# Attention and two mixture layers on one core: another order of the first tiles' sums, queries and keys, and weight splitting handed to VectorE

## The chip, the cores and the metric

The kernel runs on 1 core of one Trainium2 chip. The metric is the device time of one execution in microseconds (us), the median of several runs. The five engines named below are TensorE (PE; PEld is its weight load), VectorE (DVE), ScalarE (ACT), GpSimd (POOL) and SyncE (SP, which here only issues DMAs).

## What is computed

```python
q_pool = q.reshape(B, H, S // 2, 2, D).mean(axis=3)            # B=2, H=8, S=1152, D=64
scores = np.matmul(q_pool, k.transpose(0, 1, 3, 2)) / np.sqrt(D)
attn = np.exp(scores - scores.max(-1, keepdims=True))
attn = attn / (attn.sum(-1, keepdims=True) + 1e-09)
x = np.matmul(attn, v)                                         # (2, 8, 576, 64)
x = x.transpose(0, 2, 1, 3).reshape(B * 576, H * D)            # 1152 tokens x 512
h = x @ w_in                                                   # 512 x 2048
x = np.maximum(0.01 * h, h) @ w_out                            # 2048 x 512
p = domain_probs / (domain_probs.sum(-1, keepdims=True) + 1e-09)
out = sum(p[:, e:e+1] * (np.maximum(x @ w1[e], 0) @ w2[e]) for e in range(4))
```

All is float32. TensorE works on a rounded type, so each operand is split into a high part (a rounded copy) and a low part (what the copy left), and a product is the sum of two or three matmuls.

## The kernel before, in words

**One instruction stream for each engine, written by hand.** The program runs under a manual schedule: every engine executes its instructions in the order in which the Python code calls them, and waits on semaphores where data or a buffer is not there yet. An instruction that waits therefore holds up everything behind it on its engine.

**Attention.** There are 8 pairs (a batch and two heads), each with 9 tiles of 128 pooled queries, so 72 tiles. A tile i goes through these steps:

- S (`emit_s`): TensorE, six matmuls 128x384 (L355), or twelve in pair 0's fifth tile, which needs both heads. They fill PSUM banks 0 to 2, and there is only one such buffer: the next tile's S waits until VectorE has read this one.
- VectorE scales the scores into SBUF tile e (five buffers) and takes the row minimum in the same instruction (L358).
- ScalarE's exp, with the row sum (`emit_exp`, L364).
- VectorE's two small steps: sum + 1e-9 (`emit_sum`, L368), then the reciprocal (L372 in `emit_norm`).
- GpSimd multiplies e by it (L374); in the last two tiles VectorE does.
- T (`emit_t`): TensorE transposes e in nine blocks (L395) through banks 3 to 5, three blocks a bank; ScalarE copies each bank to th (L399) and VectorE the rest to tl (L101).
- attention times v (L422), taken from a queue by `run_av` between other work. A finished chunk of 256 or 320 queries is added up (L430, L431) into xf and split into xh and xl (L94 or L96, and L101).

TensorE transposes tile i after it has issued S of tile i+2 (from tile 6 on of tile i+3). What comes before a tile's T is `upto("sum")`; the reciprocal and the normalisation stand inside `emit_t`, behind the first third of tl.

**Keys and queries.** For pair 0 (`first_pair`), both are loaded piece by piece: q_add pools the query pairs (L257), q_hi and q_lo split them, k_hi and k_lo the keys. For later pairs (`prep_pair`), q_add (L292), k_hi, k_lo, q_hi and q_lo run on GpSimd and ScalarE some tiles ahead. GpSimd's k_lo takes one instruction rk 128x1152; behind it SyncE issues four key DMAs (L288, L289), and behind q_lo four query DMAs into qst (L304).

**Weights.** The first feed-forward layer runs over 16 slices f of w_in, 36 matmuls 128x384 each (L190 to L192), and ends in `evac_leaky` (ScalarE's leaky ReLU into gf, L589, ScalarE's high part, VectorE's low part of 128x1152). `split64` splits a slice of weights that come as 64-bit words: s0 on ScalarE (L113), s1 VectorE (L116), s2 VectorE (L120), s3 VectorE (L127), ScalarE (L128) and one subtraction (L130), s4 (L134 on VectorE or L136 on GpSimd), s5 an addition (L139). Its argument `fast` says who does these: with 0 GpSimd does L130, L136 and L139 and ScalarE one more product (L122); with 1 VectorE does L134, GpSimd L130 and L139; with 2 VectorE does all three. `prep_a` splits w_in into tiles a, `prep_b` w_out into tiles b. Slices 0 and 1 of w_in are split during the last pair's tiles (`ahead`, AT0), slice 2 after attention, slice f+2 during slice f. What follows (w_out, and the four experts) the change does not touch.

Of the kernel before, what the change touches and what calls it, by code (L numbers as in the profile page):

```python
# [27 lines left out]
CW = 384  # L28
# [10 lines left out]
def tile_kernel(ctx: ExitStack, tc: tile.TileContext, q, k, v, w_in, w_out, probs, w1, w2, out):  # L39
# [130 lines left out]
    def prep_b(f, tmp):  # L170
        h, l = b_t[f] = tuple(b_b[f % 8][:, i] for i in range(2))
        return split64(h, l, wb_raw[f % 2].rearrange("p (a b) -> p a b", b=2), tmp, 1)
# [23 lines left out]
    with ExitStack() as actx:  # L196
# [76 lines left out]
        def prep_pair(n):  # L273
# [55 lines left out]
        P0, P1, P2 = 11, 1, 8  # L329
# [3 lines left out]
        AT0 = (0, 6)  # L333
# [116 lines left out]
        with tc.manual_schedule():  # L450
# [36 lines left out]
            for c in range(3):  # L487
                k_lo(DVE, 1, c * CW, (c + 1) * CW)
# [398 lines left out]
```

## Time and profile before

| | |
|---|---|
| median of 3 runs | 844.21 us (843.22 to 845.43) |
| profiled execution | 844.05 us |
| its span, first to last instruction | 842.0 us |
| mean granted TensorE clock | 0.996 of full speed |
| PE busy | 820.8 us (97%) |
| PEld busy | 775.6 us (92%) |
| DVE busy | 574.1 us (68%) |
| ACT busy | 434.5 us (52%) |
| POOL busy | 417.3 us (50%) |
| chain that ended last | PE 89%, DVE 7%, issue 2%, ACT 1%, POOL 1%, DMA 1% |

The shares are over the whole span, and the stages differ much: the last two thirds are nearly TensorE alone. A row of a timeline reads: start, duration, engine, line, operation, tile written and tiles read, shape, how many alike in a run; in brackets the idle time of the engine before it and what ended this. Times count from the start of the span, which is 2 us less than the execution.

### The profile page before, as it was taken

The page shows a single profiled execution, that of the slowest core. Times are in us where ns is not written, and L with a number is a line of the kernel's source. Part 1 is how long each engine was busy: PE and PEld are TensorE (multiplying, and loading weights), DVE is VectorE, ACT ScalarE, POOL GpSimd, SP SyncE. Part 2 cuts the span into 40 slices and gives each one's busy share as a digit, 9 for nine tenths or more (in the row PEclk, how much of TensorE's full clock was granted, in tenths as well). Part 3 has the DMA queues.
Part 4 walks back from the last instruction along what each step waited for, and adds up shares of the span by engine and source line. Part 5 has one row for each costly group of instructions (what it writes and reads, how often), then busy time and mean ns, then how long its engine had stood idle before and what let it go on. Part 6 is the DMA issues. An engine that isn't in the chain of part 4 may idle for free.

```text
span 842.0 us, 13590 instructions
## 1 busy us (share of the span) xinstructions
PE 820.8 (97%) x5091; PEld 775.6 (92%) x5091; DVE 574.1 (68%) x947; ACT 434.5 (52%) x764; POOL 417.3 (50%) x366
## 2 busy tenths in 40 slices
PE   6899999999989899999999999999999999999998
PEld 5799999999989799999999998989898998989897
DVE  5889999999998979767765762736445363625332
ACT  5889999999976555433432641505142341506030
POOL 3788888888753678556561240506042331504020
PEclk9999999999999999999999999999999999999999
DMA  7347644563401233331130120302011110201012
GB/s 224 90 132 189 181 105 136 162 174 96 138 26 52 100 100 101 100 99 52 51 101 26 51 76 1 100 1 88 13 51 51 50 52 4 98 0 52 0 38 100
DMA packets 25713, 68.65 MB, mean 82 GB/s; under 512 B 2992, under 2 KB 7856, under 8 KB 25648
## 3 DMA queue, kind: packets, MB, share of 16 engines
q1 hardware_dynamic: 25424, 67.43, 26.8%
q8 instruction: 40, 0.66, 0.3%
q10 hardware_dynamic: 224, 0.36, 0.1%
q14 instruction: 25, 0.20, 0.1%
HBM read 48.91 MB, written 2.36 MB: 61 GB/s over the span
## 4 chain that ended last, share of the span: by engine, by line
PE 89%; DVE 7%; issue 2%; ACT 1%; POOL 1%; DMA 1%; SPq 0%; DVEq 0%; POOLq 0%; ACTq 0%
PE ps L713 21%; PE ps L355 9%; PE ps L758 8%; PE ps L760 8%; PE ps L759 8%; PE ps L422 7%; PE ps L395 7%; PE ps L612 4%; PE ps L610 4%; PE ps L611 4%; PE ps L192 3%; PE ps L191 3%; PE ps L190 3%; DVE e L358 2%; DVE tl L101 1%
## 5 line engine op out<-in xcount | busy, mean ns | idle before, releaser
L101 POOL TENSOR_TENSOR bb<-w2r,bb 128x512 fp32r<-128x512 f32 x32 | 40.8, 1297 | 259.0 <-ACT bb L94 259.0
L767 DVE SCALAR_TENSOR_TENSOR oacc<-ps,pw,oacc 128x512 f32<-128x512 f32 (+1 forms) x64 | 47.5, 742 | 100.4 <-PE ps L760 100.4
L101 DVE TENSOR_TENSOR tl<-ps,th 128x384 fp32r<-128x384 f32 (+1 forms) x240 | 112.2, 505 | 3.2 <-ACT th L399 2.8
L758 PE MATMUL ps<-bb,gg 128*128 128x512 f32 (+1 forms) x292 | 112.9, 387 | 0.0
L760 PE MATMUL ps<-bb,gg 128*128 128x512 f32 (+1 forms) x292 | 112.8, 386 | 0.0
L759 PE MATMUL ps<-bb,gg 128*128 128x512 f32 (+1 forms) x292 | 112.8, 386 | 0.0
L713 PE MATMUL ps<-yT,ws 128*128 128x288 f32 x768 | 111.3, 296 | 0.0
L374 POOL TENSOR_SCALAR e<-e,st 128x1152 f32<-128x1152 f32 x70 | 86.3, 1234 | 42.8 <-DVE st L372 25.2
L713 PEld LDWEIGHTS ps<-yT,ws 128*128 128x128 f32 x768 | 105.6, 188 | 0.9 <-ACT cb L730 0.3
L358 DVE TENSOR_SCALAR_CACHE_REDUCE e<-ps 128x1152 f32<-128x1152 f32 x72 | 97.5, 1355 | 11.0 <-PE ps L355 9.7
L355 PE MATMUL ps<-k,qst 128*128 128x384 f32 x438 | 94.4, 346 | 7.9 <-DVE e L358 3.8
L399 ACT CAST th<-ps 128x384 fp32r<-128x384 f32 (+1 forms) x240 | 91.4, 459 | 17.9 <-PE ps L395 16.3
L719 ACT COPY ca<-ps 128x576 f32<-128x576 f32 x16 | 10.3, 641 | 167.1 <-PE ps L713 155.3
L364 ACT ACTIVATE e<-e,st 128x1152 f32<-128x1152 f32 x72 | 91.3, 1268 | 4.8 <-DVE e L358 2.8
L395 PE MATMUL ps<-ident,e 128*128 128x128 f32 x648 | 83.9, 275 | 5.1 <-POOL e L374 3.4
L355 PEld LDWEIGHTS ps<-k,qst 128*128 128x128 f32 x438 | 75.6, 190 | 13.0 <-DVE e L358 6.9
L713 PE MATMUL ps<-yB,ws 128*128 128x288 f32 x576 | 84.4, 296 | 0.0
L395 PEld LDWEIGHTS ps<-ident,e 128*128 128x128 f32 x648 | 75.1, 141 | 9.7 <-POOL e L374 5.1
L713 PEld LDWEIGHTS ps<-yB,ws 128*128 128x128 f32 x576 | 79.6, 188 | 0.6
L192 PE MATMUL ps<-xh,a 128*128 128x384 f32 x192 | 65.1, 339 | 2.8 <-POOL a L139 2.8
L190 PE MATMUL ps<-xh,a 128*128 128x384 f32 x192 | 64.8, 338 | 0.7 <-ACT gf L589 0.7
L760 PEld LDWEIGHTS ps<-bb,gg 128*128 128x128 f32 x292 | 54.9, 188 | 11.4 <-DVE gg L739 0.2
(126 smaller groups left out, 1724.9 us busy)
## 6 DMA issues: line engine op xcount, KB each, us to landing
wa<-in_w_in SPq DMA_DIRECT2D x16, 512.0 KB, 3.4
wb<-in_w_out SPq DMA_DIRECT2D x16, 512.0 KB, 4.3
wf<-in_w SPq DMA_DIRECT2D x32, 256.0 KB, 2.8
w2r<-in_w SPq DMA_DIRECT2D x16, 512.0 KB, 3.4
qst<-rq SPq DMA_DIRECT2D x28, 288.0 KB, 4.6
rv<-in_v SPq DMA_DIRECT2D x8, 576.0 KB, 6.6
rk<-in_k SPq DMA_DIRECT2D x7, 576.0 KB, 6.0
rq<-in_q SPq DMA_DIRECT2D x7, 576.0 KB, 5.3
```

What stands on the lines that cost most here:

```text
L101: eng.tensor_tensor(dst, src, f32(high), op=ALU.subtract)
L190: PE.matmul(ps[:, c, :CW], wh[:, k_], src_h[:, k_, cs], start=k_ == 0, stop=False)
L192: PE.matmul(ps[:, c, :CW], wl[:, k_], src_h[:, k_, cs], start=False, stop=k_ == KD - 1)
L355: PE.matmul(ps[:, c, :CW], x, y, start=m == 0, stop=m == len(mms) - 1)
L358: DVE.tensor_scalar(e, ps[:, :, :CW], -0.5 / float(D) ** 0.5, None, op0=ALU.mult, op1=ALU.min, accum_out=st[:, 0:1])
L364: ACT.activation(e, e, AF.Exp, bias=st[:, 0:1], scale=-1.0, accum_out=st[:, 1:2])
L395: PE.transpose(ps[:, j], e[:, (3 * g + j) * 128:(3 * g + j + 1) * 128], ident)
L399: ACT.copy(h, ps[:, :, s0:s0 + w])
L713: PE.matmul(ps[:, c, :HW], w[wi][:, i, ks], y[:, yi, k, c * HW:(c + 1) * HW], start=bool(first and k == 0 and m == 0), stop=k == 1 and m = ...
L758: PE.matmul(ps, gh[:, ts_], wh, start=f == fs[0], stop=False)
L759: PE.matmul(ps, gh[:, ts_], wl, start=False, stop=False)
L760: PE.matmul(ps, gl[:, ts_], wh, start=False, stop=f == fs[-1])
```

## The change

Three parts. **The first nine tiles:** pooling, q_hi and q_lo of pair 0 are cut into 128 and 320 columns, the first of which GpSimd subtracts; q_lo of head 1 goes from VectorE to GpSimd; of head 1's three key parts two move behind tile 2's scaling; the sums and reciprocals are called earlier (`sums`, `norms`), in tiles 0, 2 and 3 ahead of the next S; pair 1 is prepared one tile earlier, its queries ahead of its keys, with q_lo and its DMAs before k_lo. **The last pair:** GpSimd normalises all tiles; each slice of w_in has a list of tiles at which its six steps are called (a negative number is a tile before the last pair); slice 2 joins the list; one dummy Lrelu loads ScalarE's table three tiles before the end. **Weights:** `prep_b` gets `fast`; slices 1 to 4 of w_in and 0 and 1 of w_out are split with fast=2. TensorE's instructions and their order are the same in both kernels.

```diff
-    def prep_b(f, tmp):
+    def prep_b(f, tmp, fast):
...
-        return split64(h, l, wb_raw[f % 2].rearrange("p (a b) -> p a b", b=2), tmp, 1)
+        return split64(h, l, wb_raw[f % 2].rearrange("p (a b) -> p a b", b=2), tmp, fast)
...
-                return [[lambda: v_hi(0)], [lambda: v_lo(0)], [], [lambda: v_hi(1)], [], [lambda: v_lo(1)]]
+                return [[lambda: v_hi(0)], [lambda: v_lo(0)], [], [], [lambda: v_hi(1)], [lambda: v_lo(1)]]
             qk = [[q_add, k_hi], [k_lo], [q_hi], [q_lo, lambda: load_qk(n + 1)]]
+            if n == 1:
+                qk = [[q_add], [k_hi, q_hi], [q_lo, k_lo, lambda: load_qk(n + 1)], [], []]
...
-        P0, P1, P2 = 11, 1, 8
+        P0, P1, P2 = 11, 0, 8
-        AT0 = (0, 6)
+        AT0 = ((-3, -2, 0, 2, 3, 4), (6, 7, 7, 8, 9, 9), (8, 10, 10, 11, 11, 11))
...
-            eng = POOL if i < len(tiles) - 2 else DVE
-            eng.tensor_scalar(e, e, st[:, 3:4], 1.0, op0=ALU.mult, op1=ALU.mult)
+            POOL.tensor_scalar(e, e, st[:, 3:4], 1.0, op0=ALU.mult, op1=ALU.mult)
...
-            q_add(POOL, 0, 128, SQ)
+            for a, z in ((128, 256), (256, SQ)):
+                q_add(POOL, 0, a, z)
+            q_hi(0, 128, 256)
             upto("s", emit_s, 0)
-            q_hi(0, 128, SQ)
+            q_lo(POOL, 0, 128, 256)
+            q_hi(0, 256, SQ)
             keep_warm(10)
             upto("exp", emit_exp, 0)
-            q_lo(DVE, 0, 128, SQ)
+            q_lo(DVE, 0, 256, SQ)
...
             upto("s", emit_s, 1)
-            for c in range(3):
-                k_lo(DVE, 1, c * CW, (c + 1) * CW)
+            k_lo(DVE, 1, 0, CW)
...
-                    ahead_a[f] = prep_a(f, tmp)
+                    ahead_a[f] = prep_a(f, tmp, 2 if f else 0)
...
-            for f, t0 in enumerate(AT0):
-                ahead.setdefault(t0, []).extend([begin(f), step(f, 0)])
-                for d, ks in enumerate([(1, 2), (3,), (4,), (5,)]):
-                    ahead.setdefault(t0 + 1 + d, []).extend([step(f, k_) for k_ in ks])
+            for f, ts in enumerate(AT0):
+                ahead.setdefault(ts[0], []).append(begin(f))
+                for k_, t in enumerate(ts):
+                    ahead.setdefault(t, []).append(step(f, k_))
...
-            begin_at = {9 * m - P0: m for m in range(3, len(pairs))} | {0: 0, P1: 1, P2: 2}
-            steps = {0: [lambda: q_hi(1, 0, SQ), lambda: q_lo(DVE, 1, 0, SQ)]}
+            begin_at = {9 * m - P0: [m] for m in range(3, len(pairs))} | {P1: [0, 1], P2: [2]}
+            steps = {0: [lambda: q_hi(1, 0, SQ), lambda: q_lo(POOL, 1, 0, SQ)]}
...
+                if i in (0, 2, 3):
+                    sums()
+                    norms()
                 upto("s", emit_s, i + lead - (i == L2))
                 if i == 0:
-
-                    upto("norm", emit_norm, i + lead - 1)
-                upto("sum", emit_sum, i + lead - 1 - (i == L2))
-                emit_t(i, lambda: upto("norm", emit_norm, i + lead - 1 - (i == L2)))
+                    for c in (1, 2):
+                        k_lo(DVE, 1, c * CW, (c + 1) * CW)
+                sums()
+                if i <= L2:
+                    norms()
+                emit_t(i, norms)
...
+                if i == len(tiles) - 3:
+
+                    ACT.activation(warm, warm, AF.Lrelu, alpha=0.01)
...
-        run(next_a(2, 2))
-        run(evac_leaky(0, f0_ps), next_a(3), next_b(0))
+        run(evac_leaky(0, f0_ps), next_a(3, 2), next_b(0, 2))
...
-        run(evac_leaky(1, ps), next_b(1))
+        run(evac_leaky(1, ps), next_b(1, 2))
...
-                run(evac_leaky(f, ps), next_a(f + 2, f == 2), *[next_b(b) for b in when_b.get(f, [])])
+                run(evac_leaky(f, ps), next_a(f + 2, 2 * (f == 2)), *[next_b(b) for b in when_b.get(f, [])])
```

How the instructions of two engines stand, before and after. First VectorE from tile 0's scores to tile 3's (e0 to e3 are the tiles' e, k10 is head 1's keys, r01 and r11 its raw keys and queries, st the small sums; lines below 330 are the same in both, L358, L368 and L372 are now L360, L370 and L374). Before:

```order
L101 TENSOR_TENSOR qst0_65<-rq_82,qst0_65 128x448
L368 TENSOR_SCALAR st_90<-st_90 128x1
L372 RECIPROCAL st_90<-st_90 128x1
L358 TENSOR_SCALAR e1_77,st_90<-ps 128x1152
L101 TENSOR_TENSOR k10_59<-r01_83,k10_59 64x384 x3
L358 TENSOR_SCALAR e2_78,st_90<-ps 128x1152
L368 TENSOR_SCALAR st_90<-st_90 128x1
L101 TENSOR_TENSOR tl0_73<-ps,th0_71 128x3x128
L372 RECIPROCAL st_90<-st_90 128x1
L101 TENSOR_TENSOR tl0_73<-ps,th0_71 128x3x128 x2
L101 TENSOR_TENSOR qst0_65<-r11_84,qst0_65 128x576
L358 TENSOR_SCALAR e3_79,st_90<-ps 128x1152
```

After the change:

```order
L101 TENSOR_TENSOR qst0_65<-rq_82,qst0_65 128x320
L370 TENSOR_SCALAR st_90<-st_90 128x1
L374 RECIPROCAL st_90<-st_90 128x1
L360 TENSOR_SCALAR e1_77,st_90<-ps 128x1152
L101 TENSOR_TENSOR k10_59<-r01_83,k10_59 64x384
L370 TENSOR_SCALAR st_90<-st_90 128x1
L374 RECIPROCAL st_90<-st_90 128x1
L360 TENSOR_SCALAR e2_78,st_90<-ps 128x1152
L101 TENSOR_TENSOR k10_59<-r01_83,k10_59 64x384 x2
L101 TENSOR_TENSOR tl0_73<-ps,th0_71 128x3x128 x3
L360 TENSOR_SCALAR e3_79,st_90<-ps 128x1152
```

Tile 1's sum and reciprocal have come ahead of tile 2's scaling, two of the three key parts have gone behind it, and head 1's 576-column q_lo is no longer here.

GpSimd from tile 1's normalisation on (L374, now L375; rq and rk are pair 1's raw queries and keys, kh1 their high part). Before:

```order
L374 TENSOR_SCALAR e1_77<-e1_77,st_90 128x1152
L374 TENSOR_SCALAR e2_78<-e2_78,st_90 128x1152
L292 TENSOR_TENSOR rq_82<-rq_82 128x576
L374 TENSOR_SCALAR e3_79<-e3_79,st_90 128x1152
L101 TENSOR_TENSOR rk_81<-rk_81,kh1_70 128x1152
L374 TENSOR_SCALAR e4_80<-e4_80,st_90 128x1152
L96 TENSOR_SCALAR xh_55<-xf_88 64x256
L101 TENSOR_TENSOR xl_56<-xf_88,xh_55 64x256
L374 TENSOR_SCALAR e0_76<-e0_76,st_90 128x1152
L101 TENSOR_TENSOR rq_82<-rq_82 128x576
L96 TENSOR_SCALAR qmid1_68<-rq_82 64x64 x2
L374 TENSOR_SCALAR e1_77<-e1_77,st_90 128x1152
```

After the change:

```order
L375 TENSOR_SCALAR e1_77<-e1_77,st_90 128x1152
L101 TENSOR_TENSOR qst0_65<-r11_84,qst0_65 128x576
L292 TENSOR_TENSOR rq_82<-rq_82 128x576
L375 TENSOR_SCALAR e2_78<-e2_78,st_90 128x1152
L375 TENSOR_SCALAR e3_79<-e3_79,st_90 128x1152
L101 TENSOR_TENSOR rq_82<-rq_82 128x576
L96 TENSOR_SCALAR qmid1_68<-rq_82 64x64 x2
L101 TENSOR_TENSOR rk_81<-rk_81,kh1_70 128x1152
L375 TENSOR_SCALAR e4_80<-e4_80,st_90 128x1152
```

Head 1's q_lo (qst0) is new here, and pair 1's q_lo (rq by L101) with its two small copies stands ahead of k_lo (rk) and of tile 4's normalisation instead of behind it by three tiles.

VectorE after attention: slice 3 of w_in (wa1, tile a0) and slice 0 of w_out (wb0, tile b0). Before:

```order
L116 TENSOR_SCALAR c1_121<-c1_121 128x512
L116 TENSOR_SCALAR c0_120<-c0_120 128x512
L120 SCALAR_TENSOR_TENSOR c1_121<-wa1_115,c1_121 128x512
L120 SCALAR_TENSOR_TENSOR c0_120<-wb0_116,c0_120 128x512
L101 TENSOR_TENSOR g0_103<-gf_113,g0_103 128x1152
L127 TENSOR_SCALAR wa1_115<-c1_121 128x512
L127 TENSOR_SCALAR wb0_116<-c0_120 128x512
L134 SCALAR_TENSOR_TENSOR wb0_116<-wb0_116 128x512
```

After the change:

```order
L116 TENSOR_SCALAR c1_121<-c1_121 128x512
L120 SCALAR_TENSOR_TENSOR c0_120<-wa1_115,c0_120 128x512
L120 SCALAR_TENSOR_TENSOR c1_121<-wb0_116,c1_121 128x512
L101 TENSOR_TENSOR g0_103<-gf_113,g0_103 128x1152
L127 TENSOR_SCALAR wa1_115<-c0_120 128x512
L130 TENSOR_TENSOR a0_92<-c0_120,a0_92 128x512
L127 TENSOR_SCALAR wb0_116<-c1_121 128x512
L130 TENSOR_TENSOR b0_95<-c1_121,b0_95 128x512
L134 SCALAR_TENSOR_TENSOR wa1_115<-wa1_115 128x512
L134 SCALAR_TENSOR_TENSOR wb0_116<-wb0_116 128x512
L139 TENSOR_TENSOR a0_92<-a0_92,wa1_115 128x512
L139 TENSOR_TENSOR b0_95<-b0_95,wb0_116 128x512
```

Two subtractions (L130), a product (L134) and two additions (L139) that GpSimd did stand on VectorE now.

## Rows read from the trace of the kernel before

**Rows 1.** The page: TensorE's busy tenths in 40 slices of 21.05 us
```profile
PE   6899999999989899999999999999999999999998
```

**Rows 2.** Timeline of TensorE at the start: start us, us, what [idle before <-releaser]
```profile
11.25 1.31 PE L355 MATMUL ps<-k,qst 128*128 128x384 f32 x6 [1.02 <-DVE qst L101]
...
17.93 1.31 PE L355 MATMUL ps<-k,qst 128*128 128x384 f32 x6 [1.61 <-DVE e L358]
...
21.94 3.18 PE L355 MATMUL ps<-k,qst 128*128 128x384 f32 x12
...
32.43 1.20 PE L395 MATMUL ps<-ident,e 128*128 128x128 f32 x9 [0.75 <-POOL e L374]
...
36.18 1.20 PE L395 MATMUL ps<-ident,e 128*128 128x128 f32 x9 [1.50 <-POOL e L374]
...
42.73 1.28 PE L355 MATMUL ps<-k,qst 128*128 128x384 f32 x6 [1.26 <-DVE tl L101]
```

**Rows 3.** Timeline of SyncE at the start
```profile
37.54 3.67 SPq L304 DMA_DIRECT2D qst<-rq  x4
```

**Rows 4.** Windows: us, busy (x instructions) by engine, granted clock, DMA share, GB/s
```profile
20.00:22.00 2.00, 1.94 (x10) 1.61 (x10) 2.00 (x5) 1.35 (x3) 0.00 (x1) 0.58 0.00 0
```

**Rows 5.** Window over the last four tiles of attention
```profile
235.00:250.00 15.00, 12.47 (x87) 11.08 (x87) 14.84 (x39) 11.63 (x28) 9.68 (x10) 1.00 0.11 36
```

**Rows 6.** Timeline of TensorE, tile 69 and slices 3 and 4
```profile
248.52 1.01 PE L395 MATMUL ps<-ident,e 128*128 128x128 f32 x6 [1.24 <-DVE tl L101]
...
277.70 0.44 PE L192 MATMUL ps<-xh,a 128*128 128x384 f32 x1 [0.99 <-POOL a L139]
...
287.68 0.44 PE L190 MATMUL ps<-xh,a 128*128 128x384 f32 x1 [0.68 <-ACT gf L589]
...
290.08 0.69 PE L192 MATMUL ps<-xh,a 128*128 128x384 f32 x1 [1.80 <-POOL a L139]
```

**Rows 7.** Windows over slices 1 to 4 of the first feed-forward layer
```profile
270.00:290.00 20.00, 16.61 (x93) 15.66 (x91) 19.83 (x18) 12.25 (x17) 13.50 (x9) 1.00 0.26 87
290.00:294.00 4.00, 3.92 (x14) 3.92 (x15) 4.00 (x5) 2.60 (x4) 2.33 (x3) 0.57 0.34 131
```

**Rows 8.** Timeline of GpSimd at the start
```profile
8.50 1.15 POOL L257 TENSOR_TENSOR rq<-rq 128x448 f32<-128x448 f32 x1 [6.36 <-DMA rq<-in_q]
...
18.77 1.23 POOL L374 TENSOR_SCALAR e<-e,st 128x1152 f32<-128x1152 f32 x1 [3.65 <-DVE st L372]
```

**Rows 9.** Timeline of VectorE at the start, and at tile 70
```profile
9.18 1.36 DVE L358 TENSOR_SCALAR_CACHE_REDUCE e<-ps 128x1152 f32<-128x1152 f32 x1 [0.71 <-PE ps L355]
...
11.96 0.15 DVE L368 TENSOR_SCALAR st<-st 128x1 f32<-128x1 f32 x1 [0.76 <-ACT e L364]
...
246.73 1.27 DVE L374 TENSOR_SCALAR e<-e,st 128x1152 f32<-128x1152 f32 x1
```

**Rows 10.** Groups of VectorE, 4 to 25 us: us, mean ns | idle before
```profile
L101 DVE TENSOR_TENSOR tl<-ps,th 128x384 fp32r<-128x384 f32 x6 | 3.1, 546 | 0.0
```

**Rows 11.** Groups of GpSimd, 0 to 45 us
```profile
L101 POOL TENSOR_TENSOR rk<-rk,kh 128x1152 fp32r<-128x1152 f32 x1 | 2.7, 2679 | 0.0
...
L101 POOL TENSOR_TENSOR rq<-rq 128x576 fp32r<-128x576 f32 x1 | 1.4, 1417 | 0.0
```

**Rows 12.** Groups of VectorE, 263.8 to 267.8 us, GpSimd idle
```profile
L130 DVE TENSOR_TENSOR a<-c,a 128x512 fp32r<-128x512 f32 x1 | 0.7, 693 | 0.3 <-ACT a L128 0.3
...
L127 DVE TENSOR_SCALAR wa<-c 128x512 int32<-128x512 int32 x1 | 0.4, 428 | 0.0
```

**Rows 13.** Groups of VectorE, 268.7 to 288.5 us
```profile
L116 DVE TENSOR_SCALAR c<-c 128x512 int32<-128x512 int32 x5 | 3.2, 640 | 1.1 <-ACT c L113 1.0
L127 DVE TENSOR_SCALAR wb<-c 128x512 int32<-128x512 int32 x2 | 3.0, 1518 | 0.0
...
L120 DVE SCALAR_TENSOR_TENSOR c<-wa,c 128x512 int32<-128x512 int32 x2 | 2.4, 1180 | 0.0
...
L134 DVE SCALAR_TENSOR_TENSOR wb<-wb 128x512 f32<-128x512 uint32 x2 | 2.1, 1052 | 0.1
```

More of the change, by code (lines that the diff above doesn't have):

```diff
@@ L510, in step, with sums, norms @@
                 return lambda: ahead_a[f][i] and ahead_a[f][i]()
-            for f, t0 in enumerate(AT0):
-                ahead.setdefault(t0, []).extend([begin(f), step(f, 0)])
-                for d, ks in enumerate([(1, 2), (3,), (4,), (5,)]):
-                    ahead.setdefault(t0 + 1 + d, []).extend([step(f, k_) for k_ in ks])
-            for t, load in [(4, load_b), (4, load_b), (AT0[0] + 5, load_a), (AT0[1] + 5, load_a)]:
+            for f, ts in enumerate(AT0):
+                ahead.setdefault(ts[0], []).append(begin(f))
+                for k_, t in enumerate(ts):
+                    ahead.setdefault(t, []).append(step(f, k_))
+            for t, load in [(4, load_b), (4, load_b), (5, load_a), (9, load_a), (12, load_a)]:
                 ahead.setdefault(t, []).append(load)
-            begin_at = {9 * m - P0: m for m in range(3, len(pairs))} | {0: 0, P1: 1, P2: 2}
-            steps = {0: [lambda: q_hi(1, 0, SQ), lambda: q_lo(DVE, 1, 0, SQ)]}
+            begin_at = {9 * m - P0: [m] for m in range(3, len(pairs))} | {P1: [0, 1], P2: [2]}
+            steps = {0: [lambda: q_hi(1, 0, SQ), lambda: q_lo(POOL, 1, 0, SQ)]}
             for i, (n, t) in enumerate(tiles):
-                if i in begin_at:
-                    for d, fs in enumerate(prep_pair(begin_at[i])):
+                for m in begin_at.get(i, []):
+                    for d, fs in enumerate(prep_pair(m)):
                         steps.setdefault(i + d, []).extend(fs)
                 lead = 2 if i < L2 else 3
+                def sums():
+                    upto("sum", emit_sum, i + lead - 1 - (i == L2))
+                def norms():
+                    upto("norm", emit_norm, i + lead - 1 - (i == L2))
+                if i in (0, 2, 3):
+                    sums()
+                    norms()
                 upto("s", emit_s, i + lead - (i == L2))
                 if i == 0:
-                    upto("norm", emit_norm, i + lead - 1)
-                upto("sum", emit_sum, i + lead - 1 - (i == L2))
-                emit_t(i, lambda: upto("norm", emit_norm, i + lead - 1 - (i == L2)))
+                    for c in (1, 2):
[4 more added lines that the diff above has]
+                emit_t(i, norms)
                 run_av(AVB.get(t, AVD) if i > L2 else AV0.get(t, AVD))
@@ L554, in tile_kernel @@
                     f()
-                if n == len(pairs) - 1:
-                    for f in ahead.get(t, []):
-                        f()
-            run_av(1e9)
-            for t in range(9, 16):
+                for f in ahead.get(i + 9 - len(tiles), []):
+                    f()
+                if i == len(tiles) - 3:
+                    ACT.activation(warm, warm, AF.Lrelu, alpha=0.01)
+            for t in range(9, 13):
                 for f in ahead.get(t, []):
                     f()
+                while t < 11 and av:
+                    cost, f = av.pop(0)
+                    f()
+                    if not cost:
+                        break
+            assert not av
             while f0:
@@ L573, in tmp, with next_b @@
         return next(ring)
[L575 to L576 removed]
+    def next_b(f, fast=1):
+        return prep_b(f, tmp, fast) + [load_b]
     def view(t, n=NC):
```

2 lines of the change are left out of this document (removed).

## The prediction, made before the changed kernel was run

> **What bounds the kernel now.** I read the page first. TensorE is busy 97% of the span and carries the chain almost alone, and its instructions do not change, so time can come only from its idle moments and from matmuls that ran at a lowered clock. The row of tenths says where these are: the first slice has 6, the second 8, then all have 9 but for the slices that begin at 231.5 and 273.6 us (8 each) and the very last [rows 1]. These are the first tiles, the end of attention and the first feed-forward slices, where the change works. So I went through TensorE's timeline in these three places for the idle time in brackets, and then through the engines it names.
>
> At the start TensorE waits again and again: for tile 1's queries (1.02), for tile 2's scaling before tile 3's scores (1.61), for GpSimd's normalisation of tiles 4 and 5 (0.75, 1.50), and before pair 1's first scores (1.26) [rows 2]. The bracket there names a tl piece, but SyncE issues pair 1's queries only from 37.54, four DMAs in 3.67 us [rows 3], and these scores read them, so I take them for that wait. Behind the early idle time the granted clock is 0.58 [rows 4], most of the stretch at the lower of its levels (1.2 of 2.4 GHz): twelve matmuls take 3.18 us, where six take 1.31 at the full clock [rows 2].
>
> Over the last four tiles TensorE is idle for 15.00 - 12.47 = 2.5 us [rows 5]; the largest piece is 1.24 [rows 6]. In the weight stage there are waits of 0.99, 0.68 and 1.80 [rows 6], and then again a stretch at clock 0.57, 4 us long [rows 7]. VectorE is busy 19.83 of the 20 us before it [rows 7].
>
> **The change, part by part. The start.** I follow tiles 1 to 4 through the new order.
> - Tile 1's scores waited for a 448-column q_lo on VectorE. Its first 128 columns now come from GpSimd, whose 448-column q_add took 1.15 [rows 8]; by columns the 128 cost some 0.4. Then the scores wait only for the bank, free when tile 0's scaling ends (9.18 + 1.36 [rows 9]): 10.6 instead of 11.25. If a small GpSimd step costs as much as the whole one, this gains nothing.
> - Tile 0's sum waits for its exp and runs at 11.96 as before, 1.4 behind the scaling [rows 9]. Tile 1's scaling follows at 12.35, tile 2's scores at 13.75. Tile 1's sum and reciprocal (0.15 each [rows 9]) come 1.4 after its scaling and end at 15.4; then tile 2's scaling starts. It must now start about 16.5 (17.93 less 1.36), behind three key parts, of which two move away. The next scores go out at 16.8, not 17.93.
> - Tile 1's normalisation can start at 15.4, not 18.77 [rows 8], so its transposes follow the scores at once.
> - VectorE then owes two key parts and three tl pieces, all of 384 columns, priced at 0.5 each [rows 10]: 16.75 + 2.5 = 19.25. Tile 3's scaling ends at 20.6, and tile 4's scores, twelve matmuls, 2.2 us at the full clock, at 22.8. They end at 21.94 + 3.18 = 25.1 now [rows 2]. The lead is 2.3 us.
> - Ahead of tile 4's normalisation GpSimd now gets pair 1's q_lo (1.42) and two small copies besides k_lo (2.68) [rows 11], which is there already. The wait of 0.75 doubles, and the lead falls to 1.75 (it need not lose all of the 2, as tile 3's normalisation comes earlier too).
> - The 1.50 goes, as q_lo and the copies are done and tile 5's reciprocal no longer stands behind a tl piece. The 1.26 goes: the query DMAs are issued at about 26, the keys' at about 30, well ahead of the scores at 38. 1.75 + 1.50 + 1.26 = 4.5; I take **4.6**, for some smaller waits.
>
> The ends are 2.7 (nothing gained at tile 1, and the 1.26 stays because the keys, now issued last, come late) and 6.1 (GpSimd's work ahead of tile 4 is hidden, so that its 0.75 goes instead of doubling).
>
> **The end of attention.** The 1.24 [rows 6] stands behind VectorE's normalisation of tile 70 (1.27 [rows 9]), ahead of two tl pieces whose banks the next transposes need. On GpSimd this normalisation has at most one addition of slice 0 (L139) ahead of it; it ends about 248.6, before TensorE comes to that tile near 250. Most of the rest stands behind two weight steps of VectorE in front of one scaling; they are now in different tiles. Of the 2.5 us I take **2.0**, between 1.2 and 2.5.
>
> **The weights.** TensorE waits for GpSimd's L139 twice [rows 6]; a slice goes from VectorE to ScalarE, GpSimd, VectorE and GpSimd again. Where both work, VectorE's steps stretch: L127 takes 0.43 with GpSimd idle [rows 12] and 1.52 in the 20 us from 268.7 [rows 13]. In that window the excess over the unstretched price (L116 0.43, as L127; L120 and L134 0.69, as L130) is 4 x 1.09 + 4 x 0.49 + 2 x 0.36 + 5 x 0.21 = 8.1 [rows 12, 13]; the two L127 and two L120 groups are alike. The change adds nine steps up to slice 4 (three for slice 3, two each for slice 4 and for both of w_out), 0.69 each [rows 12]: 6.2. With GpSimd idle throughout, the chain is 19.8 - 8.1 + 6.2 = 17.9 us. Slice 2 is now split before the last chunk ends, so slice 3 begins when ScalarE has done its part after slice 0's last matmul, about 266.4. Slice 4 is then ready at 284.3. TensorE asks for it at 290.08 - 1.80 = 288.3 now [rows 6], and at 286.6 when the two earlier waits are gone: 2.3 us of margin. Slice 3's eleven steps (7.9) end at 274.3, asked for at 277.70 - 0.99 = 276.7 [rows 6]. So all three waits go, 3.5, and with them the slow stretch, (1 - 0.57) x 4.0 = 1.7 [rows 7]. I take **5.2**; the lower end is 3.5. Were each added step as dear as the stretched L127, 1.52, and nothing else shorter, slice 4 would come far too late; that is a rival below.
>
> **What it costs.** Slice 1's four steps (0.43 + 3 x 0.69 = 2.5 [rows 12]) and two of slice 2 (1.1) now stand on VectorE around the last chunks' xf and xl, which the last matmuls of slice 0 read. I take **0.6** lost, between 0 and 1.5. The Lrelu dummy moves ScalarE's table load off the way from slice 0 to its gf; TensorE has slice 1 to work on there, so I price it at nothing.
>
> **The sum** is 4.6 + 2.0 + 5.2 - 0.6 = 11.2. From the profiled execution, 844.05 (0.16 below the median of 844.21), that leaves **832.8 us**.
>
> **Rivals.**
> 1. *The slow clock comes back in another place*, as behind tile 4's longer wait. In both stretches above it followed idle time. For it: a wait of 1.5 remains. Against it: behind the 1.50 at 36.18 the nine transposes took the usual 1.20 [rows 2]. It costs 1.7: 834.5. Chance 0.12.
> 2. *The start gains nothing*: GpSimd's short steps come late, and what lead there is goes in front of tile 4. For it: GpSimd gets 4.6 us of work there. Against it: it idles 3.65 before tile 1's normalisation now [rows 8], so it begins all of this earlier. 844.05 - 2.0 - 5.2 + 0.6 = 837.4. Chance 0.12.
> 3. *VectorE becomes the bound of the weight stage.* It is busy 99% there already [rows 7]. If its steps stay stretched (by ScalarE or the DMAs, not by GpSimd), the nine added steps cost 6.2 and nothing is given back; less the 2.3 of earlier start, today's wait of 3.5 becomes 7.4 and the slow stretch stays. With start and end gaining, 844.05 - 4.6 - 2.0 + 0.6 + 3.9 = 842.0: no change. Against it: ScalarE worked beside the short steps of [rows 12] too. Chance 0.06. The Trainium skill, "Perfetto Trace Analysis", section "Optimizing Scalar/DVE Operations", speaks against the change here: from a saturated VectorE work may better go away, even to GpSimd. By that rule the time would be this rival's. The same section adds that the two share a read port, so that moving work between them might not help; the stretched rows agree with this second half, which is why I give the first little.
> 4. *Slower: the first tiles become one serial round.* With the sum ahead of the next scaling, VectorE stands still until exp is done. Scores 1.31 [rows 2], scaling 1.36, exp 1.4, sum and reciprocal 0.3 [rows 9] make 4.4 us a tile, in which TensorE has 2.5 us of work. If it then falls to the lower clock and stays there, its 3 us or so a tile (with attention times v) double over the five or six tiles up to pair 1: about 16 lost, the other parts gained, 844.05 + 16 - 6.6 = 853.5. It decides if tile 2's scaling starts later than today's 16.5. For it: the sum waits 0.76 today [rows 9]. Against it: the order is so only in tiles 0, 2 and 3, and the waits replace key parts that took as long. Chance 0.04.
>
> That the change does not do what it says can be left out: the order of VectorE and GpSimd shows the moves.
>
> **How the numbers follow.** The forecast has 0.66. Its ends come from the parts: at best 6.1 + 2.5 + 5.2 - 0 = 13.8 (830.3), at worst 2.7 + 1.2 + 3.5 - 1.5 = 5.9 (838.2). The runs of before lie about 1 us to either side, so the range is 829.3 to 838.2; it holds rivals 1 and 2 and leaves out 3, 4 and the forecast's tails. Within 0.3% (2.5 us, what a measurement can tell) is rival 3, 0.06; slower is rival 4, 0.04; faster the rest, 0.90.
>
> **What the changed profile would show.** Right: 9 tenths in the slices at 231 and 273 us; the clock at 1.00 there, with no wait above 0.5 for a weight slice; VectorE's L127 at 0.43; pair 1's first scores at about 38; one wait near 1.5 for tile 4's normalisation. Wrong: a clock below 1 in a stretch after 20 us; VectorE's steps at 1.5 with GpSimd idle; tile 2's scaling later than 16; a wait on pair 1's keys.

## The result, and the profile after

The changed kernel takes 834.3 us, the median of 4 runs (833.6 to 835.54), beside 844.5 (843.22 to 845.43) for the kernel before: a ratio of 0.9879, 95% interval 0.9866 to 0.9892, or 10.2 us less. The profiled execution is the longest of the four, 835.54 us with a span of 833.7, which is 8.3 less than the 842.0 before. A second profile of the same kernel, taken beside its parts, has a span of 833.1.

The busy tenths of TensorE now show 9 in the two later slices that had 8 [rows 1]; the first two, with 6 and 8, and the very last, with 8, are as they were.

```profile
PE   6899999999999999999999999999999999999998
```

TensorE's instructions are the same in both kernels, so each matmul can be set against itself. The lead, its start before less its start after, shows where the time came from:

| place (start before) | first profile: start, lead | second profile: start, lead | forecast lead |
|---|---|---|---|
| pair 1's first scores (42.73) | 41.69, 1.04 | 40.79, 1.94 | 4.6 |
| tile 69, second bank (248.52) | 245.31, 3.21 | 244.48, 4.05 | 6.6 |
| slice 0, last low part (263.37) | 260.63, 2.74 | 259.78, 3.59 | 6.0 |
| slice 4, back at full clock (293.13) | 284.81, 8.32 | 283.96, 9.17 | 11.2 |
| last matmul | 8.22 | 8.81 | 11.2 |

From row to row the end of attention gave 2.2 and 2.1 (forecast 2.0), slice 0 cost 0.5 (0.6), the weight stage gave 5.6 in both (5.2). The start gave 1.0 and 1.9, not 4.6.

The timeline of TensorE at the start, in the first profile of the change (columns as in [rows 2], whose waits these lines answer):

```profile
8.82 2.12 PE L357 MATMUL ps<-k,qst 128*128 128x384 f32 x6 [2.85 <-DVE k L101]
...
12.68 1.31 PE L357 MATMUL ps<-k,qst 128*128 128x384 f32 x6
...
18.48 1.32 PE L357 MATMUL ps<-k,qst 128*128 128x384 f32 x6 [0.73 <-DVE e L360]
...
22.33 2.38 PE L357 MATMUL ps<-k,qst 128*128 128x384 f32 x12 [0.72 <-DVE e L360]
...
32.82 1.93 PE L396 MATMUL ps<-ident,e 128*128 128x128 f32 x9 [1.74 <-POOL e L375]
34.41 2.27 PE L357 MATMUL ps<-k,qst 128*128 128x384 f32 x6
...
41.69 1.23 PE L357 MATMUL ps<-k,qst 128*128 128x384 f32 x6
```

The wait of 1.61 ahead of tile 3's scores is 0.73, and the 1.50 at tile 5 and the 1.26 ahead of pair 1's scores are gone; SyncE issues the query DMAs, which these scores read, from 28.18 and not from 37.54 [rows 3]:

```profile
28.18 3.71 SPq L304 DMA_DIRECT2D qst<-rq  x4
```

But three things were not in the sum. The first scores began at 8.82 and not at 7.58, as the DMA that brings their keys let ScalarE's k_hi start at 7.66 and not at 6.42; and these six matmuls, 1.56 us in the profile before, took 2.12. Before the change, and then ScalarE after it:

```profile
6.42 1.34 ACT L94 CAST k<-rk 128x384 fp32r<-128x384 f32 x3 [2.35 <-DMA rk<-in_k]
7.58 1.56 PE L355 MATMUL ps<-k,qst 128*128 128x384 f32 x6 [1.59 <-DVE k L101]
```

```profile
7.66 1.34 ACT L94 CAST k<-rk 128x384 fp32r<-128x384 f32 x3 [3.62 <-DMA rk<-in_k]
```

The wait for tile 4's normalisation was 1.74, not 1.5. And behind it tile 4's transposes took 1.93 and the next scores 2.27, at the lower clock, as the windows of the same profile show (columns as in [rows 4]); the last two lines are the last four tiles and slices 1 to 3, which answer to [rows 5, 7]:

```profile
30.00:34.00 4.00, 2.26 (x13) 1.93 (x13) 2.91 (x8) 2.05 (x5) 3.92 (x5) 0.89 0.98 222
34.00:36.00 2.00, 2.00 (x9) 2.00 (x8) 1.83 (x6) 1.80 (x6) 1.15 (x1) 0.50 0.95 253
232.00:247.00 15.00, 14.68 (x107) 13.56 (x106) 14.71 (x41) 13.80 (x32) 12.33 (x13) 1.00 0.04 12
263.00:283.00 20.00, 20.00 (x117) 20.00 (x116) 17.93 (x30) 12.63 (x17) 0.00 (x0) 1.00 0.39 132
```

Over the last four tiles TensorE is idle for 0.3, not 2.5. In the weight stage it has no gap in 20 us, at clock 1.00, and GpSimd does nothing there. The groups of VectorE in that stretch (answering to [rows 13]):

```profile
L116 DVE TENSOR_SCALAR c<-c 128x512 int32<-128x512 int32 x4 | 1.7, 424 | 0.4 <-ACT c L113 0.2
...
L120 DVE SCALAR_TENSOR_TENSOR c<-wa,c 128x512 int32<-128x512 int32 x2 | 1.4, 688 | 0.0
...
L130 DVE TENSOR_TENSOR a<-c,a 128x512 fp32r<-128x512 f32 x2 | 1.4, 686 | 0.0
...
L134 DVE SCALAR_TENSOR_TENSOR wb<-wb 128x512 f32<-128x512 uint32 x2 | 1.4, 684 | 0.0
...
L127 DVE TENSOR_SCALAR wb<-c 128x512 int32<-128x512 int32 x2 | 0.8, 423 | 0.0
```

L127 is back at 0.42, L120 at 0.69, and each of the added steps costs 0.69. From slice 3's first L116 (263.04) to the end of slice 4's last addition (280.15) it is 17.1 us; the forecast had 17.9.

### The profile page after: what moved, and what is told of

The parts are those of the page before. It is cut to its first block, busy times and chain, and to the rows that moved or that the text cites. A ratio compares the mean times of both kernels' runs of the same rounds, so it can differ in the third digit from the quotient of the medians.

```text
span 833.7 us, 13590 instructions
## 1 busy us (share of the span) xinstructions
PE 820.1 (98%) x5091; PEld 776.0 (93%) x5091; DVE 567.6 (68%) x956; ACT 433.6 (52%) x764; POOL 405.3 (49%) x359
## 4 chain that ended last, share of the span: by engine, by line
PE 89%; DVE 7%; issue 2%; POOL 1%; DMA 1%; ACT 0%; SPq 0%; DVEq 0%; POOLq 0%; ACTq 0%
PE ps L737 21%; PE ps L784 8%; PE ps L782 8%; PE ps L783 8%; PE ps L357 8%; PE ps L423 7%; PE ps L396 6%; PE ps L191 4%; PE ps L634 4%; PE ps L190 4%; PE ps L192 4%; PE ps L636 4%; PE ps L635 4%; DVE e L360 3%; DVE tl L101 2%
## 5 line engine op out<-in xcount | busy, mean ns | idle before, releaser
L101 POOL TENSOR_TENSOR bb<-w2r,bb 128x512 fp32r<-128x512 f32 x32 | 40.8, 1297 | 258.7 <-ACT bb L94 230.7
L101 DVE TENSOR_TENSOR tl<-ps,th 128x384 fp32r<-128x384 f32 (+1 forms) x240 | 111.8, 505 | 4.3 <-ACT th L400 3.9
L375 POOL TENSOR_SCALAR e<-e,st 128x1152 f32<-128x1152 f32 x72 | 88.8, 1234 | 35.5 <-DVE st L374 20.7
L360 DVE TENSOR_SCALAR_CACHE_REDUCE e<-ps 128x1152 f32<-128x1152 f32 x72 | 97.5, 1354 | 8.4 <-PE ps L357 7.2
L784 PEld LDWEIGHTS ps<-bb,gg 128*128 128x128 f32 x292 | 54.8, 188 | 11.4 <-DVE gg L763 0.2
L783 PEld LDWEIGHTS ps<-bb,gg 128*128 128x128 f32 x292 | 54.8, 188 | 10.6
L782 PEld LDWEIGHTS ps<-bb,gg 128*128 128x128 f32 x292 | 54.8, 188 | 10.5
```

What stands on the lines that cost most here:

```text
L101: eng.tensor_tensor(dst, src, f32(high), op=ALU.subtract)
L360: DVE.tensor_scalar(e, ps[:, :, :CW], -0.5 / float(D) ** 0.5, None, op0=ALU.mult, op1=ALU.min, accum_out=st[:, 0:1])
L375: POOL.tensor_scalar(e, e, st[:, 3:4], 1.0, op0=ALU.mult, op1=ALU.mult)
L782: PE.matmul(ps, gh[:, ts_], wh, start=f == fs[0], stop=False)
L783: PE.matmul(ps, gh[:, ts_], wl, start=False, stop=False)
L784: PE.matmul(ps, gl[:, ts_], wh, start=False, stop=f == fs[-1])
```

## The experiments

Theory: the three parts work by the forecast's mechanisms, and what is missing of the start is late keys, a lowered clock at tile 0 and a slow stretch behind tile 4. Rivals stand with each run.

**The parts, each alone on the kernel before.** The first run has only the new order of the first nine tiles, the second only the last pair's edits, the third only the weights (slice 1's three steps that went to VectorE are in none of the three):

```diff
         run(next_a(2, 2))
-        run(evac_leaky(0, f0_ps), next_a(3), next_b(0))
+        run(evac_leaky(0, f0_ps), next_a(3, 2), next_b(0, 2))
-        run(evac_leaky(1, ps), next_b(1))
+        run(evac_leaky(1, ps), next_b(1, 2))
-                run(evac_leaky(f, ps), next_a(f + 2, f == 2), *[next_b(b) for b in when_b.get(f, [])])
+                run(evac_leaky(f, ps), next_a(f + 2, 2 * (f == 2)), *[next_b(b) for b in when_b.get(f, [])])
```

> Only the first nine tiles changed. Theory: the new order works as forecast, and what was missing in the profile of the change (1.04 us of lead at pair 1's first scores, not 4.6) is two things: the first keys landed 1.24 us later in that execution, and the long wait for tile 4's normalisation (1.74) is followed by matmuls at the lower clock, worth 1.8. Then the lead against tile 0's scaling is 2.8 with a slow stretch behind tile 4, 4.6 without, and the time 840 to 842. Rival: the start is worth only the 1.0 seen, whatever the landing: 843.5.

> Only the last pair changed: GpSimd normalises all tiles, slice 2 is split ahead. Theory: 2.2 us at the end of attention (idle 2.5 falls to about 0.3), and slice 3 begins 2.3 earlier, which takes as much from the waits of 3.5 in the weight stage: 840.0, and 838.3 if the slow stretch at slice 4 goes with them. Rival: the waits in the weight stage are GpSimd's and VectorE's stretched steps and stay as long: 842.3.

> Only the splitting of slices 3 and 4 of w_in and 0 and 1 of w_out moved to VectorE, slice 2 still after attention. Theory: with GpSimd idle VectorE's steps shrink to their short times (L127 0.43), its chain to slice 4 shrinks by 2 although it has nine more steps, slice 4 is ready as TensorE asks for it, and all of 3.5 and the slow stretch of 1.7 go: 839.3. Rival: VectorE is the bound, its steps stay stretched, the nine cost 6.2 more: 848 or above.

> The changed kernel once more, beside its parts. Theory: 834.3 again; with the first keys landing at 7.6, not 8.8, pair 1's first scores come 1.2 to 1.8 earlier than in the first profile. If the start, tail and weight parts were independent, their gains alone would add up to its 10.2; as tail and weights both take the same waits at slices 3 and 4, I expect their sum to be 2 to 4 larger. Rival: the sum is 10.2.

Beside 844.23 for the kernel before, the start alone takes 841.43 (ratio 0.9967, 0.9956 to 0.9978), the last pair alone 839.78 (0.9945, 0.993 to 0.996), the weights alone 839.97 (0.9951, 0.9935 to 0.9966), and the whole change 834.86 (0.9885, 0.9871 to 0.99). Each of the three parts lies at its theory and not at its rival. (The start, counted from tile 0's scaling, brings pair 1's scores 2.9 earlier, with the slow stretch behind tile 4 in its profile.) The gains are 2.8, 4.45 and 4.26, in sum 11.5; together they give 9.4. So the times overlap by 2.1, at the low end of what was expected; but the four intervals together leave about 2.4 either way on that difference (an estimate from them), so the times alone do not put out the rival, a sum without overlap. The traces do. Between slice 0's last low part and slice 4 (the table's third and fourth rows) the last pair's edits alone gain 4.2, the weights alone 5.7, and the whole change 5.6: both take the same waits of slices 3 and 4. With the last pair's edits alone one wait is left there, with the weights alone none. TensorE in the run with the last pair's edits, and a window of the run with the weights:

```profile
285.62 0.45 PE L192 MATMUL ps<-xh,a 128*128 128x384 f32 x1 [1.02 <-POOL a L139]
```

```profile
270.00:290.00 20.00, 20.00 (x117) 20.00 (x116) 19.83 (x33) 14.17 (x19) 2.06 (x1) 1.00 0.33 114
```

The second profile of the whole change again has the wait of 1.74 and the slow stretch; keys that come 0.9 earlier make pair 1's scores 0.9 earlier:

```profile
7.93 2.12 PE L357 MATMUL ps<-k,qst 128*128 128x384 f32 x6 [2.46 <-DVE k L101]
...
31.89 2.02 PE L396 MATMUL ps<-ident,e 128*128 128x128 f32 x9 [1.74 <-POOL e L375]
33.56 2.19 PE L357 MATMUL ps<-k,qst 128*128 128x384 f32 x6
...
40.79 1.23 PE L357 MATMUL ps<-k,qst 128*128 128x384 f32 x6
```

The start alone shows two things more of the slow clock. Its lead of 1.90 at pair 1's scores falls to 0.3 behind the end of attention, where the old wait of 1.24 is still in place and is now followed by a slow stretch, which the kernel before did not have there. And in the weight stage, which this run leaves as it was, the old wait ahead of slice 4 is followed by the full clock, where the kernel before had 0.57 [rows 7]; that alone brings some 1.4:

```profile
248.00:250.00 2.00, 2.00 (x9) 2.00 (x8) 1.46 (x3) 0.88 (x2) 0.00 (x0) 0.50 0.09 35
290.00:292.00 2.00, 2.00 (x13) 2.00 (x13) 2.00 (x3) 1.38 (x4) 0.64 (x1) 1.00 0.63 172
```

```profile
289.74 0.45 PE L192 MATMUL ps<-xh,a 128*128 128x384 f32 x1 [1.78 <-POOL a L139]
```

**What the clock hangs on.** Three runs change one thing each at the start. The first calls tile 3's sum and reciprocal ahead of the values' low part; the second fills TensorE's wait at tile 4; the third warms up longer:

```diff
+                if i == 1:
+                    upto("sum", emit_sum, 3)
+                    upto("norm", emit_norm, 3)
                 for f in steps.get(i, []):
```

```diff
+                if i == 4:
+                    for _ in range(14):
+                        PE.transpose(PS[:, 7, :128], ident, ident)
                 emit_t(i, norms)
```

```diff
-            keep_warm(20)
+            keep_warm(30)
```

> The change, with tile 3's sum and reciprocal called at the end of tile 1, ahead of VectorE's low part of the first values (1.24 us). Theory: the wait of 1.74 for tile 4's normalisation goes back to GpSimd standing idle 1.0 before tile 3's, for a reciprocal behind that low part; now it starts 1.0 earlier, the wait falls to 0.7, the matmuls behind it keep the full clock, and pair 1's first scores come 2.5 to 2.8 earlier: 832.2. Rival: the slow stretch behind tile 4 is due to the early waits, not this one, and stays: 833.9. Second rival: something else of tile 4 ends last and nothing moves.

> The change, with 14 transposes of the identity into an unused bank on TensorE ahead of tile 4's transposes (1.5 us of work in a wait of 1.74). Theory: the clock fell because TensorE stood still there; with this filling tile 4's transposes start where they did but take 1.15, not 1.9 to 2.0, the next scores 1.25, not 2.2, and pair 1's first scores come 1.7 to 2.0 earlier: 833.0. Rival: the clock falls for something else (the early waits, or no reason in TensorE's activity), and the time stays at 834.8 or grows.

> The change, with 30 warm-up transposes, not 20, while the first keys are on their way. Theory: in three of the four profiles where the keys came at 7.9 or later, tile 0's six matmuls took 2.12 at the lower clock, where the profile with the keys at 7.6 has 1.56; kept busy, TensorE does them in 1.5, tile 0's scaling starts 0.6 earlier, and all of the start with it: 834.2. Rival: the ten transposes end behind the keys and cost what they bring, or the clock does not rise: 834.8.

They take 833.73 (ratio 0.9879, 0.9864 to 0.9894), 833.99 (0.9883, 0.9868 to 0.9898) and 833.51 (0.9879, 0.9862 to 0.9895), beside 843.83 for the kernel before; against the change itself the intervals overlap, so the traces must tell. TensorE with the wait filled:

```profile
29.83 1.69 PE L552 MATMUL ps<-ident 128*128 128x128 f32 x14
31.77 1.20 PE L396 MATMUL ps<-ident,e 128*128 128x128 f32 x9 [0.25 <-POOL e L375]
32.72 1.32 PE L357 MATMUL ps<-k,qst 128*128 128x384 f32 x6
...
39.55 1.20 PE L357 MATMUL ps<-k,qst 128*128 128x384 f32 x6
```

The transposes of tile 4 start where they did and take 1.20, the scores 1.32: with work in the wait the clock held in this execution. Pair 1's scores come 1.24 earlier than in the second profile of the change, of which the earlier keys account for 0.13, and not 1.7 to 2.0: tile 5's transposes, 1.45 earlier, now start as tile 5's normalisation ends. GpSimd in the first profile of the change, idle ahead of tile 3's normalisation, and then with tile 3's reciprocal moved:

```profile
25.51 1.24 POOL L375 TENSOR_SCALAR e<-e,st 128x1152 f32<-128x1152 f32 x1 [1.03 <-DVE st L374]
```

```profile
22.79 2.97 POOL L375 TENSOR_SCALAR e<-e,st 128x1152 f32<-128x1152 f32 x2
...
30.55 1.23 POOL L375 TENSOR_SCALAR e<-e,st 128x1152 f32<-128x1152 f32 x1
```

Tiles 2 and 3 are normalised back to back in 2.97, not 2.46, and tile 4's starts at 30.55, with 1.30 of TensorE's wait left, not 0.7. The clock stays full in this profile, so the first rival's slow stretch is not there; but the time, 833.73, is nearer to that rival's 833.9 than to the theory's 832.2, as half of the expected gain is missing. With the longer warm-up:

```profile
7.76 1.56 PE L357 MATMUL ps<-k,qst 128*128 128x384 f32 x6
...
31.16 1.20 PE L396 MATMUL ps<-ident,e 128*128 128x128 f32 x9 [1.75 <-POOL e L375]
32.12 1.30 PE L357 MATMUL ps<-k,qst 128*128 128x384 f32 x6
...
38.97 1.23 PE L357 MATMUL ps<-k,qst 128*128 128x384 f32 x6
```

```profile
28.00:32.00 4.00, 2.25 (x17) 1.88 (x16) 3.26 (x10) 1.93 (x6) 3.92 (x4) 1.00 0.98 219
32.00:36.00 4.00, 3.88 (x27) 3.24 (x26) 3.56 (x11) 4.00 (x13) 1.57 (x3) 1.00 1.00 252
```

Tile 0's scores take 1.56 again, as expected. The wait at tile 4 is as long as ever, 1.75, and yet the clock holds behind it. Pair 1's scores have a lead of 3.76 over the kernel before, and the last matmul 10.9. Nor is the warm-up the reason. Two runs below have the change's own instructions up to the last tiles, with 20 warm-up transposes: in the run with GpSimd at work (the first two lines) the clock holds behind the same wait, in the run with VectorE's two normalisations (the last line) it falls.

```profile
33.34 1.20 PE L396 MATMUL ps<-ident,e 128*128 128x128 f32 x9 [1.75 <-POOL e L375]
34.30 1.32 PE L357 MATMUL ps<-k,qst 128*128 128x384 f32 x6
```

```profile
32.09 1.86 PE L397 MATMUL ps<-ident,e 128*128 128x128 f32 x9 [1.77 <-POOL e L376]
```

So a wait of 1.74 to 1.77 is followed by the lower clock in four profiles (of the change, twice, of the start alone, and with VectorE's normalisations) and by the full clock in two. The same instructions come out both ways; what decides it is open. It also means that one profile each does not show that the filling, or the shorter wait, kept the clock up. Of the change's eight executions four have the mean granted clock of its two profiles, 0.996 (834.61 to 835.86 us), and four 0.998 (833.6 to 834.79), which fits a stretch that comes in some executions only; the latter have no trace.

**Who stretches VectorE's steps.** The change, with GpSimd kept at work behind the last chunk:

```diff
+        dum = g_b[8][:, 0, :512]
+        for _ in range(16):
+            POOL.tensor_tensor(dum, f32(xl[:, KD - 1, NT - 512:]), f32(xh[:, KD - 1, NT - 512:]), op=ALU.subtract)
         run(evac_leaky(0, f0_ps), next_a(3, 2), next_b(0, 2))
```

> The change, with 16 subtractions of 128x512 added on GpSimd from the end of attention on, whose result nothing reads before it is overwritten; TensorE, VectorE and ScalarE do the same as before. Theory: it is GpSimd that stretches VectorE's weight steps; L127 goes back from 0.42 to 1.5, L120 and L134 to 1.2 to 1.7, VectorE's chain to slice 4 grows by 8 to 12, and TensorE waits for slices 3 and 4 again: 840 to 846. Rival: the steps were short because of their new order or because ScalarE does less beside them; then GpSimd's work changes nothing: 834.8.

It takes 849.5 us (ratio 1.0063, 1.0048 to 1.0078), 15 more than the change. VectorE, GpSimd and TensorE in it:

```profile
274.00 1.48 DVE L127 TENSOR_SCALAR wa<-c 128x512 int32<-128x512 int32 x1
275.40 1.76 DVE L130 TENSOR_TENSOR a<-c,a 128x512 fp32r<-128x512 f32 x1
...
260.05 26.33 POOL L799 TENSOR_TENSOR g<-xl,xh 128x512 fp32r<-128x512 f32 x16 [7.42 <-DVE xl L101]
...
285.31 0.69 PE L192 MATMUL ps<-xh,a 128*128 128x384 f32 x1 [9.34 <-DVE a L139]
```

Each of GpSimd's instructions takes 26.33 / 16 = 1.65, and VectorE's steps follow each other at about the same pace from 260 to 287, when GpSimd is done; then L127 is 0.42 again. Slice 3's addition comes so late that TensorE waits 9.34, and behind that wait it runs at half the clock until 290:

```profile
286.00:290.00 4.00, 4.00 (x14) 4.00 (x14) 3.97 (x6) 1.26 (x2) 0.38 (x1) 0.50 0.81 246
```

The mechanism is the one expected, and the rival is out, as nothing but GpSimd's work was added. The size is 3.5 above its upper end: I had taken the excess of the profile before, where GpSimd was busy for 13.50 of 20 us [rows 7] and not throughout, and had no term for that slow clock, which costs 2.3 between slice 3 and slice 4 (the lag behind the first profile of the change grows from 11.4 to 13.7).

**VectorE's last two normalisations.**

```diff
-            POOL.tensor_scalar(e, e, st[:, 3:4], 1.0, op0=ALU.mult, op1=ALU.mult)
+            eng = POOL if i < len(tiles) - 2 else DVE
+            eng.tensor_scalar(e, e, st[:, 3:4], 1.0, op0=ALU.mult, op1=ALU.mult)
```

> The change, with VectorE normalising the last two tiles as before. Theory: of the 2.2 us won at the end of attention, the 1.24 hangs on this alone; it comes back, in front of two thirds of tile 69's transposes, and the lead of TensorE over the kernel before falls from 4.0 to 2.8 there: 836.0. Rival: the weight steps' new places made VectorE early enough to hide the normalisation: 834.7, as the change.

It takes 835.78 (ratio 0.9902, 0.9887 to 0.9917), and the wait is back in its old place:

```profile
245.78 1.01 PE L397 MATMUL ps<-ident,e 128*128 128x128 f32 x6 [1.24 <-DVE tl L101]
```

Against the second profile of the change TensorE falls back by 1.31 there and keeps that to the end. So the trace puts the rival out; the time alone, with its interval, would not.

**The edits together.** Beside the longer warm-up and the earlier reciprocal, pair 1's q_add goes ahead of head 1's q_lo on GpSimd, and slice 2's second and third step behind the last xl:

```diff
-                qk = [[q_add], [k_hi, q_hi], [q_lo, k_lo, lambda: load_qk(n + 1)], [], []]
+                qk = [[], [k_hi, q_hi], [q_lo, k_lo, lambda: load_qk(n + 1)], [], []]
...
-        AT0 = ((-3, -2, 0, 2, 3, 4), (6, 7, 7, 8, 9, 9), (8, 10, 10, 11, 11, 11))
+        AT0 = ((-3, -2, 0, 2, 3, 4), (6, 7, 7, 8, 9, 9), (8, 11, 11, 11, 11, 11))
...
+            def q_add1():
+                rq = raw[1][1]
+                POOL.tensor_tensor(rq[:, 0], rq[:, 0], rq[:, 1], op=ALU.add)
+
-            steps = {0: [lambda: q_hi(1, 0, SQ), lambda: q_lo(POOL, 1, 0, SQ)]}
+            steps = {0: [lambda: q_hi(1, 0, SQ), q_add1, lambda: q_lo(POOL, 1, 0, SQ)]}
```

> The change with four small edits: 30 warm-up transposes; tile 3's sum and reciprocal ahead of the values' low part; pair 1's q_add on GpSimd ahead of head 1's q_lo, in the 1.9 us in which GpSimd waits for ScalarE; slice 2's second and third step behind the last chunk's xl. Theory: 0.5 from tile 0's matmuls at the full clock, 0.5 or a little more from a shorter wait at tile 4, 1.8 in those executions in which the slow stretch stood behind it, 0.4 at the last matmuls of slice 0: 831.6. Rival: VectorE is full from 14 to 30 us, so that what is won ahead of tile 4 is waited for right behind it: 833.3.

It takes 832.31 us (831.99 to 832.38; ratio 0.986, 0.9843 to 0.9876), 0.7 above the theory and 1.0 below the rival, and each of its runs is below each of the change's. TensorE:

```profile
7.95 1.56 PE L357 MATMUL ps<-k,qst 128*128 128x384 f32 x6 [1.52 <-DVE k L101]
...
30.56 1.20 PE L396 MATMUL ps<-ident,e 128*128 128x128 f32 x9 [1.08 <-POOL e L375]
31.52 1.30 PE L357 MATMUL ps<-k,qst 128*128 128x384 f32 x6
...
38.37 1.23 PE L357 MATMUL ps<-k,qst 128*128 128x384 f32 x6
```

Its leads over the kernel before are 4.36 at pair 1's scores, 6.23 at tile 69, no loss in slice 0, and 11.45 at the last matmul. It is the fastest version I have.

## Why the prediction was right, and where it was not

The forecast was 832.8 us, the measured median is 834.3, inside the range and faster as said. Point by point:

- **The start's chain was right up to tile 4.** Counted from tile 0's scaling (9.18 in the forecast, 10.97 measured), tile 2's scaling should start 6.2 later (measured 17.08, 6.1), tile 3's 10.1 later (20.92, 9.95), and tile 4's scores end 13.6 later (24.71, 13.7). VectorE waited for exp, 0.8 to 0.9 twice, and no serial round followed (rival 4):

```profile
16.81 0.15 DVE L370 TENSOR_SCALAR st<-st 128x1 f32<-128x1 f32 x1 [0.83 <-ACT e L366]
17.08 1.34 DVE L360 TENSOR_SCALAR_CACHE_REDUCE e<-ps 128x1152 f32<-128x1152 f32 x1
```

- **The step that failed is the term of the start, 4.6**, which measured 1.04 and 1.94. Three things are missing. First, it took the keys' arrival from one execution. The first scores began at 7.58 there; in the other eleven profiles they began between 7.72 and 8.82. In the seven profiles with the new order and 20 warm-up transposes, where TensorE had stood idle for 2.26 to 2.85 before them, these matmuls also took 1.67 to 2.29, not 1.56; with 30 warm-up transposes both profiles have 1.56. Together this makes tile 0's scaling 1.8 and 0.9 late in the change's two profiles. What the old order makes of late keys is not shown: the run with only the last pair's edits had its first scores 0.46 late and was still 0.43 late at tile 3's scores; its lag went at tile 4, where its twelve matmuls took 2.38 at the full clock and not 3.18.
- **Second, rival 1 came true** in both profiles of the change: the slow stretch behind tile 4. It was given 0.12 and 1.7 us. Counted from tile 0's scaling, the four profiles with this stretch lead at pair 1's scores by 2.8 to 2.9, the filled wait and the longer warm-up, without it, by 3.9 to 4.0: it cost some 1.1. (The run with GpSimd at work, also without it, has 3.4, but lost 0.4 already ahead of tile 1's scaling.) As the same instructions run with it and without it, nothing here tells when it comes.
- **Third, the rest**: without late keys and without the stretch the start is worth 3.9 to 4.0, so 0.6 to 0.7 of the 4.6 was never there. Some 0.3 of it is the wait at tile 4. In the version with all edits the start measures 4.36.
- **The wait at tile 4** was forecast at 1.5 and is 1.74, for the reason given (q_lo, copies and k_lo ahead of it on GpSimd). Something was not counted: tile 3's reciprocal stands behind the values' low part on VectorE, so that GpSimd idles 1.0; calling it earlier takes the wait to 1.30.
- **The 1.26 ahead of pair 1's scores** was right: the query DMAs are issued from 28.18, and the wait is gone. Keys last did not make a new one.
- **The range's upper end** lacks the 1 us that the lower end has for the runs of before; it would be 839.2, and nothing hangs on it.
- **The end of attention** (2.0, measured 2.1 to 2.2) and its reason were right; the run with VectorE's normalisations shows 1.3 of it.
- **Slice 0's cost** (0.6, measured 0.5) was right in size, but I put it to slice 1's four steps and two of slice 2. The version that moves slice 2's two steps has none, with slice 1's steps where they were. So it is those two alone. Slice 1's steps on VectorE even save something: the run with only the last pair's edits, where GpSimd still does three of them, loses 0.9, and VectorE's first xl takes 1.51 beside GpSimd there, 0.49 in the change.
- **The weights** (5.2, measured 5.6) came as worked out in what regards the waits: nine steps more, a shorter chain, and no wait left, which is 4.1 of the 5.6 (forecast 3.5). The other 1.5 is the slow stretch at slice 4, which the forecast took to go with the waits. That was in part luck: in the run with only the start changed the waits stand and the stretch is gone all the same, so it does not hang on the waits alone. Rival 3 fell: with GpSimd idle VectorE's steps were at their short times in spite of ScalarE and the DMAs, and with GpSimd busy they stretched. The rule in the Trainium skill, "Perfetto Trace Analysis", section "Optimizing Scalar/DVE Operations", that a saturated engine may want work taken off it, even to GpSimd, would have spoken for the kernel before. Its second half, on the shared port, is what the runs bear out: the weights alone, work taken from GpSimd to a VectorE that was 99% busy, gained 4.26 us.

## What to carry to other kernels

Before work is moved off a busy engine, compare the same instruction's time with the other engine idle and busy: if it stretches beside the other, part of the busy share is waiting, and bringing the work back can shorten the chain. A term that starts from a DMA's arrival should be priced over several executions, and so should a slow stretch of the clock: here it came and went with the same instructions, so that one profile with it and one without show neither what brought it nor what removed it.

## What was not expected of the hardware

With GpSimd reading SBUF without a pause, it and VectorE took turns: 1.65 us for each of GpSimd's 16 instructions, and VectorE's weight steps, 0.42 or 0.69 alone, all 1.5 to 1.8, the one-input L127 as well as the two-input L130. The Trainium skill, "SBUF — State Buffer", section "Who interferes with whom", says that the only contention is for one port pair that the two share, an exclusive lock; that a VectorE instruction with two SBUF inputs contends with a GpSimd instruction that reads SBUF; and that in VectorE's two-port modes the loser waits for the whole instruction. The trace agrees for the two-input steps (1.76 for L130), and adds that neither starves, since they alternate; whether the one-input L127, at 1.48, ran in a two-port mode no run shows. And the granted clock did not follow from the length of a wait alone: 1.74 to 1.77 us at tile 4 was followed by half the clock in four profiles, and 1.75 by the full clock in two others, one of them of the same instructions.
